# Outer products of the last two pairs of tiles as seven block products, with sums kept in SBUF and three PSUM banks

## The chip, the cores and the metric

The program runs on one core of one Trainium2 chip. The metric is the device time in microseconds (us) of a whole execution. The kernel before took 988.21 us, the median of three runs (985.57 to 989.87).

## The reference

The input is q, k and v of an attention with 8 batches, 8 heads, 576 positions and 64 features per head, and three weight matrices. Keys and values are averaged over groups of 8 positions, so each query sees 72 keys. The attention's output, reshaped to 4608 tokens of 512 features, goes through a gated layer:

```
attn_out = softmax(q @ mean8(k).T / 8) @ mean8(v)      # per head
x = attn_out.transpose(0, 2, 1, 3).reshape(4608, 512)
a = x @ w_a            # 512 -> 1536
b = x @ w_b            # 512 -> 1536
out = (a * b) @ w_out  # 1536 -> 512
```

All is float32. Nearly all of the multiplications lie in the last three lines.

## The kernel before

The 4608 tokens are nine tiles of 512 (`NT`). The 1536 gated features are twelve blocks of 128 (`NF`, index f). Every float32 operand of a matmul is split into a rounded high part and a low part, and a product is three matmuls: high by high, low by high and high by low.

Tiles 0 to 2 are computed one by one. Tiles 3 to 8 form three pairs, (3, 4), (5, 6) and (7, 8), called pairs 0, 1 and 2 here. Within a pair the products x @ w_a and x @ w_b for both tiles are done together by the scheme of Winograd: `both(p, f)` makes seven block products for feature block f (`product`, six matmuls of 512 columns each) in three PSUM banks, and `fold` and `fold_second` combine them. VectorE does five additions and multiplications that read PSUM, ScalarE does two copies out of PSUM, and GpSimd does one addition and one multiplication. The result is a*b for the block f of the first tile (`first`) and of the second (`fifth`).

The outer product (a*b) @ w_out is the plain one in all pairs. For the first tile, `split_gated` parts the gated block into high and low, and `ffn_out` adds four groups of three matmuls into the banks acc0 to acc3; these groups stand between the block products of the next f (`rest`). The gated blocks of the second tile are written to DRAM (`later`). When the pair is through, twelve `ffn_out` of the second tile follow, 144 matmuls, with the blocks fetched back (`fetch_gated`). The sums of x that the next pair needs (`sums_of_x`) are made at that time.

The whole program is put in order at build time. `Schedule` holds chains of operations with estimated durations and ranks. It always starts the operation that can start first, and of those that can start within a small slack the one with the lowest rank. Each engine then runs its queue strictly in that written order, and semaphores hold an instruction back until what it needs is there. DMAs are all issued by SyncE. The lines that issue the work are line 292 (matmuls), 234 (additions and multiplications of VectorE and GpSimd), 256 and 260 (copies of ScalarE) and 271 (DMAs).

Four large SBUF buffers (w0 to w3) hold what is streamed in by `loads`: the block weights of one f (`stream`, tile name j, 1.8 MB in four DMAs), x of the next pair, and w_out for the second tile (tile name wo). A buffer is reused in the order in which it comes free.

Of the kernel before, what the change touches and what calls it, by code (L numbers as in the profile page):

```python
# [19 lines left out]
P = 128  # L20
# [19 lines left out]
BY_HEAD, LESS_MAX, COPIED = range(3)  # L40
EARLY = [BY_HEAD, LESS_MAX, BY_HEAD, LESS_MAX, COPIED, BY_HEAD, BY_HEAD, BY_HEAD]
# [156 lines left out]
def attn_moe_kernel(ctx: ExitStack, tc: tile.TileContext, q, k, kn, v, vn, vr, wa, wb, wo, out):  # L198
# [78 lines left out]

    def pe(calls, rank=None, turn=False):
# [67 lines left out]
    streamed = {("o", t1 * NF + f) for _, t1 in PAIRS for f in range(NF)}  # L346
    stream, combos, temps = {}, {}, []
    jd = [dram.tile([P, 2, NJ + 1, HALF * P], F32, name=f"jd{f}") for f in range(NF)]
    od = [dram.tile([P, 2, DM], F32, name=f"od{f}") for f in range(NF)]
    xd = {t: dram.tile([P, NK, NT], F32, name=f"xd{t}") for t in range(2, NTILE)}  # L350
# [48 lines left out]
    for p, (t0, t1) in enumerate(PAIRS):  # L399
        order += [("both", p, f) for f in range(NF)] + [("rest", p, 0)]  # L400
        order += [("out", t1, f) for f in range(NF)]
    lasting = {"in": 24 * 0.228, "out": 12 * 0.228, "both": 54 * 0.228, "rest": 8 * 0.228}
    due, at = {}, 28.0
    for item in order:
        if item[:2] == ("in", 0):
            at = max(at, 28.0 + 11.5 * item[2])
        due[item] = at
        at += lasting[item[0]]
    ends = {}
# [4 lines left out]
    stored |= {t1 * NF + f for _, t1 in PAIRS for f in range(NF)}  # L414
    uses, upcoming = [], {name: [] for name in ("ab", "o", "h")}
    for kind, t, f in order:
        if kind == "out":
            uses.append(t * NF + f)
        elif kind == "both":
# [218 lines left out]
    def loads():  # L638
        todo = [("x", 0)]
        for p, (t0, t1) in enumerate(PAIRS):  # L640
            todo += [("both", p, f) for f in range(NF)] + [("wo", t1, 0)]
            todo += [("x", p + 1)] if p + 1 < len(PAIRS) else []
            todo += [("wo", t1, c) for c in (1, 2)]
# [4 lines left out]
        for kind, at, *more in todo:  # L648
            tag = yield from take(free_w)
            if kind == "both":  # L650
# [7 lines left out]
                sch.spawn(freed(tag, ("product", at, f, S4)), 0.0)  # L658
            elif kind == "wo":
# [22 lines left out]
    def sums_of_x(p):  # L682
        yield W(("x", p))
        if p:
            yield W(("pair", p - 1))
# [5 lines left out]
        sch.spawn(all_temps(p, two), 0.0)  # L691
        rank = due["both", p, 0] - 12.0
        lead = rank - (SOON if not p else 0.0)
# [28 lines left out]
    def all_temps(p, two):  # L722
        if not temps:
            yield W(("split", "h", STD * NF - 1))
            yield from take(hs)
        temps[:] = [x[:, c * NT:(c + 1) * NT] for x in two for c in range(2)]
        temps.extend(place(sb, [P, NT], F32, tag, f"temp_{tag}_{p}") for tag in ("p2", "h"))
        mark("temps", p)
# [452 lines left out]
    def fold(p, f, u, v, r, first, third, fourth, fifth):  # L1181

        t0 = PAIRS[p][0]
        yield W(("product", p, f, X00))
        if f > 1:
            yield W(("split", "h", t0 * NF + f - 2))
        else:
# [28 lines left out]
        yield from split_gated(t0 * NF + f, first)  # L1216
        mark("folded", p, f)

    def fold_second(p, f, third, fourth, fifth):
# [6 lines left out]
        mark("second", p, f, 1)  # L1226
        later[x] = dram.tile([P, NT], F32, name=f"later_{x}")
        yield dma(later[x], fifth)
        mark("stored", x)

    waiting = []

    def both(p, f):
# [9 lines left out]
        first, third, fourth, fifth = temps[f % 2], temps[2], temps[3], temps[4 + f % 2]  # L1243
# [14 lines left out]
        def rest(n):  # L1258
            if f > 1 or f == 1 and n > 1:
                yield from waiting.pop(0)  # L1260

# [4 lines left out]
        if not f:  # L1266
# [7 lines left out]
        yield from product(u, A1, X01, start=False)  # L1274
        yield before_r
        yield from product(r, T3, S3)
        yield from rest(1)
        yield W(("fold", p, f, 1))
        yield from product(v, T1, S1)
        yield W(("fold", p, f, 2))  # L1280
        yield from product(r, T4, X11)
        yield from rest(2)
        yield W(("fold", p, f, 3))
        yield from product(v, B1, S4, start=False)
        yield from rest(3)
        waiting.extend(ffn_out(t0, f, (c,)) for c in range(NT // P))
# [22 lines left out]
    def main():  # L1309
        yield W(("first_ins",))  # L1310
        for kind, t, f in order:
# [9 lines left out]
            elif kind == "rest":  # L1321
# [3 lines left out]
                mark("pair", t)  # L1325

    with tc.manual_schedule():
# [18 lines left out]
        for kind, t, f in order:  # L1346
# [10 lines left out]
            elif kind == "both":  # L1357
                sch.spawn(load_weight("o", x), due[kind, t, f])
# [6 lines left out]
        sch.spawn(more_tmps(), 0.0)  # L1365
# [55 lines left out]
```

## Time and profile before

| | |
|---|---|
| median of three runs | 988.21 us |
| the profiled execution's own time | 987.53 us |
| its span, first to last instruction | 985.7 us |
| TensorE (PE) busy | 968.0 us, 98% |
| VectorE (DVE) busy | 560.6 us, 57% |
| ScalarE (ACT) busy | 387.9 us, 39% |
| GpSimd (POOL) busy | 126.4 us, 13% |
| mean granted TensorE clock | 0.997 |
| moved by DMA | 255.66 MB, 259 GB/s |

The busy time of an engine is the sum of its instructions, overlaps counted once. The chain that ended last names, step by step, what the work that came last was waiting for. Times in rows are microseconds from the span's start. Pair 0 runs from about 412 to 620 us, pair 1 from 620 to 800 us and pair 2 from 800 to 982 us. In each, the first 144 to 170 us are the block products with the first tile's outer product, and the last 36 us are the second tile's outer product.

### The profile page before, as it was taken

The numbers are of one execution on the slowest core, as the hardware profiler recorded it, in microseconds if no ns is written. First come the engines' busy times: TensorE is split into PE (matmuls) and PEld (weight loads), VectorE is DVE, ScalarE is ACT, GpSimd is POOL, SyncE is SP. The second block draws the span as 40 slices with busy tenths as digits, with TensorE's granted clock in tenths as the row PEclk, the third lists the DMA queues.
The fourth block names the chain that finished last, engine by engine and source line by source line (L and its number), as shares of the span: only waits on it lengthen the run. The fifth ranks groups of instructions, "written<-read, shape, count | busy, mean of one in ns | idle before, by whom it ended". The sixth has DMA issues, their size and how long they took to land.

```text
span 985.7 us, 12862 instructions
## 1 busy us (share of the span) xinstructions
PE 968.0 (98%) x4568; PEld 801.7 (81%) x4568; DVE 560.6 (57%) x928; ACT 387.9 (39%) x796; POOL 126.4 (13%) x109
## 2 busy tenths in 40 slices
PE   6899999999999999999999999999999999999998
PEld 5688888888888888888888878888888878888876
DVE  6898899888587943858433356333333923333331
ACT  5788666454565533644321133211111621111131
POOL 1002000000000000011212223222222212222210
PEclk9899999999999999999999999999999999999999
DMA  7798999999889998587566876766668967666791
GB/s 269 263 313 295 300 329 295 322 321 319 296 296 305 308 311 279 167 283 237 171 197 215 270 261 230 240 214 216 216 214 303 362 216 234 210 225 210 239 349 74
DMA packets 120655, 255.66 MB, mean 259 GB/s; under 512 B 10192, under 2 KB 26576, under 8 KB 120592
## 3 DMA queue, kind: packets, MB, share of 16 engines
q1 hardware_dynamic: 120592, 254.84, 77.3%
q8 instruction: 36, 0.59, 0.2%
q14 instruction: 27, 0.22, 0.1%
HBM read 195.30 MB, written 59.51 MB: 258 GB/s over the span
## 4 chain that ended last, share of the span: by engine, by line
PE 92%; DMA 4%; ACT 2%; DVE 1%; issue 1%; SPq 0%; ACTq 0%
PE acc L292 29%; PE bank_psb L292 15%; PE bank_psa L292 10%; PE bank_att L292 10%; PE psb L292 9%; PE psa L292 9%; PE po L292 4%; PE psc L292 4%; PE ptr L289 1%; PE pvp L292 1%; DMA j<-jd 1%; DMA jd<-sums_high 1%; DMA kraw<-in_kn 1%; DMA q<-in_q 0%; DMA vraw<-in_vn 0%
## 5 line engine op out<-in xcount | busy, mean ns | idle before, releaser
L292 PE MATMUL bank_psb<-x,j 128*128 128x512 f32 x648 | 165.3, 390 | 0.7 <-DMA j<-jd 0.7
L292 PEld LDWEIGHTS bank_psb<-x,j 128*128 128x128 f32 x648 | 121.0, 188 | 26.3 <-DVE temp L234 1.1
L292 PE MATMUL acc<-jo_later,hh 128*128 128x512 f32 x384 | 122.3, 400 | 0.3
L292 PE MATMUL bank_att<-x,j 128*128 128x512 f32 x432 | 110.4, 391 | 0.0
L292 PE MATMUL bank_psa<-x,j 128*128 128x512 f32 x432 | 110.2, 390 | 0.0
L292 PE MATMUL psb<-xh,jab 128*128 128x512 f32 x288 | 100.7, 398 | 0.0
L234 DVE TENSOR_TENSOR temp<-bank_psb,temp 128x512 f32<-128x512 f32 x72 | 49.8, 692 | 89.1 <-PE bank_psb L292 88.8
L292 PE MATMUL psa<-xh,jab 128*128 128x512 f32 x288 | 99.4, 398 | 0.8 <-ACT vdiag L256 0.8
L292 PEld LDWEIGHTS bank_psa<-x,j 128*128 128x128 f32 x432 | 80.8, 188 | 16.8
L292 PEld LDWEIGHTS bank_att<-x,j 128*128 128x128 f32 x432 | 80.6, 188 | 16.7
L234 DVE TENSOR_TENSOR temp<-bank_psa,temp 128x512 f32<-128x512 f32 x54 | 37.3, 691 | 90.2 <-PE bank_psa L292 89.6
L234 DVE TENSOR_TENSOR temp<-bank_att,temp 128x512 f32<-128x512 f32 x54 | 37.3, 692 | 88.8 <-PE bank_att L292 88.2
L292 PEld LDWEIGHTS acc<-jo_later,hh 128*128 128x128 f32 x384 | 69.8, 188 | 13.9 <-ACT hh L256 1.6
L292 PE MATMUL acc<-jo_later,hl 128*128 128x512 f32 x192 | 75.4, 393 | 0.2 <-DVE hl L234 0.2
L234 POOL TENSOR_TENSOR temp_p<-temp_p,temp 128x512 f32<-128x512 f32 x36 | 46.8, 1301 | 217.2 <-ACT temp_p L256 212.4
L256 ACT CAST hh<-temp 128x512 fp32r<-128x512 f32 x36 | 22.4, 623 | 128.9 <-DVE temp L234 128.9
L234 POOL TENSOR_TENSOR temp_h<-temp_h,temp 128x512 f32<-128x512 f32 x36 | 46.9, 1303 | 181.4 <-ACT temp_h L256 175.3
L292 PEld LDWEIGHTS psa<-xh,jab 128*128 128x128 f32 x288 | 54.1, 188 | 12.6 <-ACT vdiag L256 1.7
L292 PEld LDWEIGHTS psb<-xh,jab 128*128 128x128 f32 x288 | 54.1, 188 | 10.7
L292 PE MATMUL acc<-jo_open,hh 128*128 128x512 f32 x192 | 61.6, 402 | 0.4 <-ACT s L264 0.4
L292 PE MATMUL psb<-xl,jab 128*128 128x512 f32 x144 | 56.3, 391 | 0.0
L292 PE MATMUL psa<-xl,jab 128*128 128x512 f32 x144 | 56.2, 390 | 0.0
(144 smaller groups left out, 1608.6 us busy)
## 6 DMA issues: line engine op xcount, KB each, us to landing
j<-jd SPq DMA_DIRECT2D x108, 512.0 KB, 5.5
jo_later<-od SPq DMA_DIRECT2D x48, 512.0 KB, 3.8
wo<-od SPq DMA_DIRECT2D x36, 512.0 KB, 7.0
jab<-jd SPq DMA_DIRECT2D x34, 512.0 KB, 6.2
jd<-jab SPq DMA_DIRECT2D x24, 512.0 KB, 4.9
back<-later SPq DMA_DIRECT2D x43, 256.0 KB, 5.9
out<-y SPq DMA_DIRECT2D x36, 256.0 KB, 6.0
j<-jd SPq DMA_DIRECT2D x36, 256.0 KB, 4.4
```

The source lines that it names most:

```text
L234: run = lambda e: vec[e].tensor_tensor(out=out, in0=in0, in1=in1, op=op)
L256: return act(out, in_, lambda: nc.scalar.copy(out, in_), rank)
L289: nc.tensor.transpose(to, lhs, rhs)
L292: nc.tensor.matmul(to, lhs, rhs, start=start, stop=stop, skip_group_check=bool(skip))
```

## The change

For pairs 1 and 2 (`PAIRED_OUT`) the outer product is also done for both tiles at once by seven block products, over two feature blocks (2j and 2j+1) at a time. Pair 0 stays as it was.

- The weights: in the time of pair 0, `sums_of_pairs` reads w_out back, forms four sums of its blocks for each of the six j, parts them into high and low and stores them in DRAM (`wd`). In pairs 1 and 2 `loads` streams them, seven DMAs for each j (tile name w), through the same four buffers.
- The gated blocks: `sums_of_gated` makes four sums out of the gated blocks of both tiles and two f, and parts seven of them into high and low (tile names combos), by ScalarE and VectorE.
- The matmuls: `out_piece` does one block product for one half (m) of the output features, three matmuls. There are 14 such pieces for each j. Weights are the stationary operand, so the outputs come out transposed, and the host transposes them back. In even f nothing stands between the block products of `both`; in odd f up to two pieces stand behind each.
- The sums over j: three of the 14 pieces are summed in the banks acc0, acc1 and acc2. The other eleven alternate between two banks, and `add_piece` adds each to a sum in SBUF (VectorE; for j = 0 ScalarE copies).
- The end of a pair: `give_pair` forms the outputs with 14 additions and stores them.
- Gone in pairs 1 and 2: `split_gated`, the way of the second tile's gated block through DRAM, the 144 matmuls behind the pair, and the wait of the next pair's `sums_of_x` for the pair before.

In matmuls, each of the two pairs had 288 for the outer product (24 groups of 12) and now has 252 (6 times 14 times 3).

The core of the diff:

```diff
+PAIRED_OUT = 1, 2
+PAIR_MARGIN, GIVE_MARGIN = 0.5, 6.0
...
 def sums_of_x(p):
         yield W(("x", p))
-        if p:
+        if p and p - 1 not in PAIRED_OUT:
             yield W(("pair", p - 1))
...
             if not p:
                 yield W(*free_at.get(home[c], [last_in]))
+            elif p - 1 in PAIRED_OUT:
+                yield W(("product", p - 1, NF - 1, c))
...
+    out_order = [(c, m) for c in (X00, S2, X01, S3, S1, X11, S4) for m in range(2)]
+    kept_banks = {(X01, 0): "acc0", (X01, 1): "acc1", (X11, 0): "acc2"}
...
+    def sums_of_pairs():
...
+            yield tt(w0, w0, other, ALU.add, (SV, SG), rank)
...
+            yield tt(w1, w1, other, ALU.add, (SV, SG), rank)
+            yield tt(other[:, low], w0[:, high], w0[:, low], ALU.subtract, (SV, SG), rank)
+            yield tt(other[:, high], w1[:, high], w0[:, high], ALU.subtract, (SV, SG), rank)
+            yield tt(w0[:, low], w1[:, high], other[:, low], ALU.subtract, (SV, SG), rank)
+            yield tt(w0[:, high], w1[:, low], w0[:, low], ALU.subtract, (SV, SG), rank)
+            for n, x in enumerate((other, w0)):
+                hi, lo = four[:, 2 * n], four[:, 2 * n + 1]
+                yield copy(hi, x, rank)
+                yield low_part(lo, x, hi, (SV, SG), rank)
...
+    def sums_of_gated(p, j):
...
+        yield tt(s1, x10, x11, ALU.add)
+        yield tt(s2, s1, x00, ALU.subtract)
+
+        def parted(c, src):
+            slot = yield from take(combo_slots)
+            yield copy(slot[0], src)
+            yield low_part(slot[1], src, slot[0])
...
+        yield from parted(X00, x00)
+        yield from parted(S2, s2)
+        yield from parted(X01, x01)
+        yield tt(x10, x00, x10, ALU.subtract)
+        yield from parted(S3, x10)
+        yield tt(x01, x01, s2, ALU.subtract)
+        yield from parted(S1, s1)
+        yield from parted(X11, x11)
+        yield from parted(S4, x01)
...
+    def out_piece(p, j, c, m):
+        yield W(("gated", p, j, c))
...
+        if kept:
+            to, start, stop = lasts[c, m], not j, j == NF // 2 - 1
+        else:
+            tag = yield from take(pair_banks)
+            to, start, stop = bank(tag, f"pair_{p}_{j}_{c}_{m}"), True, True
+        yield pe([(to, w[:, 0], hi, start, False), (to, w[:, 0], lo, False, False), (to, w[:, 1], hi, False, stop)])
...
+    def add_piece(p, j, c, m, src, tag):
+        at = sums_at[c, m]
+        if j:
+            yield W(("added", p, j - 1, c, m))
+            yield tt(at, src, at, ALU.add)
+        else:
+            yield copy(at, src)
+        pair_banks.append(tag)
...
+    def give_pair(p, m):
...
+            yield tt(at[to], at[x], at[y], ALU.add, (SV,) if in_psum(at[x]) else (SV, SG))
...
     def both(p, f):
...
+        def piece():
+            for _ in range(1 if (p, f) == (len(PAIRS) - 1, NF - 1) else 2):
+                if p in PAIRED_OUT and pieces and pieces[0][0] <= p * NF + f:
+                    yield from pieces.pop(0)[1]
...
         yield from product(u, A0, X00)
+        yield from piece()
         yield before_v
         yield from product(v, T2, S2)
+        yield from piece()
...
+        if p in PAIRED_OUT:
+            if f % 2:
+                lag = 3 if f == 1 and p - 1 in PAIRED_OUT else 2
+                pieces.extend((p * NF + f + lag, out_piece(p, f // 2, c, m)) for c, m in out_order)
+            return
...
-        sch.spawn(more_tmps(), 0.0)
+        sch.spawn(attention_over(), 0.0)
+        sch.spawn(sums_of_pairs(), 0.0)
+        sch.spawn(late_places(), 0.0)
```

How the written order changes is shown at three places. The first is TensorE's queue in pair 2, from the fourth block product of f = 3 on. Before, a group of the first tile's outer product (acc) stands between the block products (bank):

```order
L292 MATMUL bank_psb<-x_3_5416,j_3_5729 128x512 [waits DVE_49]
L292 MATMUL bank_psb<-x_3_5416,j_3_5729 128x512 x5
L292 MATMUL bank_psa<-x_2_5476,j_3_5729 128x512 [waits DMAHW5_49,DVE_49]
L292 MATMUL bank_psa<-x_2_5476,j_3_5729 128x512 x5
L292 MATMUL acc_0_5737<-jo_later,hh_5842 128x512 [waits DMAHW4_49]
L292 MATMUL acc_0_5737<-jo_later,hh_5842 128x512
L292 MATMUL acc_0_5737<-jo_later,hl_5843 128x512
L292 MATMUL bank_psb<-x_6_5499,j_3_5729 128x512 [waits Activation_49]
L292 MATMUL bank_psb<-x_6_5499,j_3_5729 128x512 x5
```

After, at the turn from f = 8 to f = 9 of the same pair, where pair_3_... are pieces of j = 3:

```order
L300 MATMUL bank_psb<-x_3_6912,j_8_7701 128x512 [waits DVE_49]
L300 MATMUL bank_psb<-x_3_6912,j_8_7701 128x512 x5
L300 MATMUL bank_att_4119<-x_2_6932,j_8_7701 128x512 [waits DMAHW7_49,DVE_49]
L300 MATMUL bank_att_4119<-x_2_6932,j_8_7701 128x512 x5
L300 MATMUL bank_psb<-x_6_6952,j_8_7701 128x512 [waits Activation_49]
L300 MATMUL bank_psb<-x_6_6952,j_8_7701 128x512 x5
L300 MATMUL bank_att_4119<-x_0_6828,j_9_7888 128x512 [waits DMAHW7_49,DVE_49]
L300 MATMUL bank_att_4119<-x_0_6828,j_9_7888 128x512 x5
L300 MATMUL pair_3_0_0_7919<-combos_work,w_3_7765 128x512 [waits DMAHW0_49]
L300 MATMUL pair_3_0_0_7919<-combos_work,w_3_7765 128x512 x2
L300 MATMUL pair_3_0_1_7923<-combos_work,w_3_7765 128x512 x3
```

In an even f the block products now follow each other with nothing between them; in an odd f they have two pieces behind each.

The second place is VectorE's queue at the turn from pair 1 to pair 2 in the new kernel, when TensorE is in block f = 0 of pair 2. Here combos are the parted gated blocks of pair 1, late_p, late_h and s_2_0 are the fold of pair 2, and x_6 is the part of x for the seventh block product. Before, this queue held only the five operations of the fold here:

```order
L234 TENSOR_TENSOR temp_2_6565<-bank_psb,temp_2_6565 128x512 [waits PE_49,Activation_49]
L234 TENSOR_TENSOR temp_2_6566<-bank_att_4112,temp_2_6565 128x512 [waits DVE_49,PE_49]
L234 TENSOR_TENSOR temp_2_6566<-bank_att_4112,temp_2_6566 128x512 [waits DVE_49,PE_49]
L234 TENSOR_TENSOR temp_2_6565<-bank_psb,temp_2_6565 128x512 [waits PE_49]
L234 TENSOR_TENSOR temp_2_6565<-bank_psa,temp_2_6565 128x512 [waits DVE_49]
```

Now it holds:

```order
L237 TENSOR_TENSOR s_2_0_6966<-bank_psb,s_2_0_6966 128x512 [waits PE_49,Activation_49]
L237 TENSOR_TENSOR hl_1_5_6978<-hh_1_5_6977,kv_1_10_6734 128x512 [waits DVE_49]
L237 TENSOR_TENSOR combos_jo<-kv_1_10_6734,combos_jo 128x512 [waits Activation_49]
L237 TENSOR_TENSOR late_p_5502<-bank_att_4119,s_2_0_6966 128x512 [waits DVE_49,PE_49]
L237 TENSOR_TENSOR combos_jo<-hl_1_5_6978,combos_jo 128x512 [waits Activation_49]
L237 TENSOR_TENSOR combos_x_5755<-tmp_1_11_6818,combos_x_5755 128x512 [waits Activation_49]
L237 TENSOR_TENSOR late_h<-bank_att_4119,late_p_5502 128x512 [waits DVE_49,PE_49]
L237 TENSOR_TENSOR tmp_1_10_6735<-kv_1_10_6734,tmp_1_10_6735 128x512
L237 TENSOR_TENSOR x_6_6952<-x_6596,x_6_6952 128x512
L237 TENSOR_TENSOR combos_x_5755<-tmp_1_10_6735,combos_x_5755 128x512 [waits Activation_49]
```

The part x_6, without which the seventh block product can't run through, now stands behind the fold's fourth result and a sum of gated blocks.

The third place is the end of VectorE's queue. Before, its last instructions part the second tile's gated blocks, and the ends of the outputs are copied out by ScalarE:

```order
L234 TENSOR_TENSOR hl_7822<-back_7760,hh_7821 128x512 [waits DMAHW4_49,PE_49,Activation_49]
L234 TENSOR_TENSOR jo_later<-back_7786,jo_later 128x512 [waits DMAHW7_49,PE_49,Activation_49]
L234 TENSOR_TENSOR hl_7860<-back_7804,hh_7859 128x512 [waits DMAHW0_49,PE_49,Activation_49]
L234 TENSOR_TENSOR jo_later<-back_7823,jo_later 128x512 [waits DMAHW3_49,PE_49,Activation_49]
L234 TENSOR_TENSOR hl_7892<-back_7841,hh_7891 128x512 [waits DMAHW5_49,PE_49,Activation_49]
```

After, it ends with the adding of the last pieces (pair_5_...) and the additions of `give_pair`:

```order
L237 TENSOR_TENSOR sums_tmp_5786<-pair_5_2_1_8315,sums_tmp_5786 128x512 [waits PE_49]
L237 TENSOR_TENSOR sums_work<-last_acc_5789,sums_work 128x512
L237 TENSOR_TENSOR sums_tmp_5787<-pair_5_6_0_8321,sums_tmp_5787 128x512 [waits PE_49]
L237 TENSOR_TENSOR sums_tmp_5788<-pair_5_6_1_8326,sums_tmp_5788 128x512 [waits PE_49]
L237 TENSOR_TENSOR sums_tmp_5782<-sums_tmp_5782,sums_work 128x512 [waits DVE_49]
L237 TENSOR_TENSOR sums_work<-sums_work,sums_q_5784 128x512 [waits DVE_49]
L237 TENSOR_TENSOR sums_q_5784<-sums_q_5784,sums_tmp_5782 128x512 [waits DVE_49]
L237 TENSOR_TENSOR sums_tmp_5782<-last_acc_5791,sums_tmp_5782 128x512 [waits DVE_49]
L237 TENSOR_TENSOR sums_tmp_5787<-sums_tmp_5787,sums_work 128x512
L237 TENSOR_TENSOR sums_work<-last_acc_5790,sums_work 128x512 [waits Pool_49]
```

Eleven additions now stand behind the last one that waits for TensorE. From the end of the last block product of pair 2 on, TensorE's new queue holds 22 pieces and VectorE's holds 44 instructions.

## Rows read from the trace of the kernel before

**Rows 1.** The page: busy time of the engines, and the shares of the chain that ended last.

```profile
PE 968.0 (98%) x4568; PEld 801.7 (81%) x4568; DVE 560.6 (57%) x928; ACT 387.9 (39%) x796; POOL 126.4 (13%) x109
...
PE 92%; DMA 4%; ACT 2%; DVE 1%; issue 1%; SPq 0%; ACTq 0%
```

**Rows 2.** Busy time by stretch: us, then PE, PEld, DVE, ACT and POOL busy (instructions), PE's granted clock, DMA share, GB/s. The stretches are pair 0, then the block products and the second tile's outer product of pair 1, the beginning of pair 2, its block products, its outer product, and the end.

```profile
424.00:584.00 160.00, 159.90 (x758) 132.74 (x756) 74.23 (x123) 43.37 (x91) 31.63 (x24) 1.00 0.70 230
...
640.00:764.00 124.00, 124.00 (x547) 102.21 (x545) 42.30 (x62) 18.45 (x31) 25.90 (x20) 1.00 0.71 232
764.00:800.00 36.00, 35.90 (x157) 29.21 (x157) 23.53 (x31) 17.51 (x27) 6.47 (x4) 1.00 0.78 284
800.00:816.00 16.00, 15.26 (x68) 12.37 (x67) 4.84 (x7) 3.12 (x6) 2.57 (x2) 1.00 0.94 315
...
830.00:946.00 116.00, 115.89 (x511) 95.47 (x510) 39.60 (x58) 17.57 (x30) 25.92 (x20) 1.00 0.71 237
946.00:982.00 36.00, 35.98 (x156) 28.99 (x156) 8.56 (x13) 10.97 (x19) 0.00 (x0) 1.00 0.46 167
982.00:985.70 3.70, 0.00 (x0) 0.00 (x0) 0.00 (x0) 0.59 (x1) 0.00 (x0) 1.00 0.60 226
```

**Rows 3.** The chain that ended last, in order of time (start, us, what): the first block product of pair 1, a group of three outer matmuls, the waits at the ends of the pairs, and the last step.

```profile
619.64 1.36 PE bank_psa L292 x6
621.00 1.36 PE bank_psb L292 x6
...
759.98 0.69 PE acc L292 x3
...
764.19 36.12 PE acc L292 x156
...
803.98 7.81 DMA j<-jd
...
945.86 36.13 PE acc L292 x156
981.99 0.02 issue
982.01 0.59 ACT y L260
```

**Rows 4.** VectorE in order of time at the end of pair 1: start, duration, instruction, and in brackets what it waited for. The second row uses the first row's result; the fourth and fifth are independent of what stands before them.

```profile
762.07 0.69 DVE L234 TENSOR_TENSOR temp<-bank_psb,temp 128x512 f32<-128x512 f32 x1 [1.30 <-PE bank_psb L292]
762.79 0.69 DVE L234 TENSOR_TENSOR temp<-bank_att,temp 128x512 f32<-128x512 f32 x1
764.17 0.69 DVE L234 TENSOR_TENSOR hl<-temp,hh 128x512 fp32r<-128x512 f32 x1 [0.69 <-ACT hh L256]
764.78 0.69 DVE L234 TENSOR_TENSOR hl<-back,hh 128x512 fp32r<-128x512 f32 x1
765.38 0.69 DVE L234 TENSOR_TENSOR jo_later<-back,jo_later 128x512 fp32r<-128x512 f32 x1
```

**Rows 5.** Groups of instructions, shapes kept apart: line, engine, operation, out<-in, count, busy us, mean ns of one, idle before.

```profile
L234 POOL TENSOR_TENSOR temp_h<-temp_h,temp 128x512 f32<-128x512 f32 x36 | 46.9, 1303 | 181.4 <-ACT temp_h L256 175.3 <-DVE temp L234 6.1
...
L256 ACT CAST hh<-temp 128x512 fp32r<-128x512 f32 x36 | 22.4, 623 | 128.9 <-DVE temp L234 128.9
...
L234 DVE TENSOR_TENSOR sums_low<-wab,sums_low 128x256 f32<-128x256 f32 x24 | 10.2, 424 | 0.7
...
L256 ACT COPY temp<-bank_att 128x512 f32<-128x512 f32 x18 | 10.6, 588 | 4.6 <-PE bank_att L292 4.3
```

**Rows 6.** VectorE and GpSimd (POOL) at work at the same time on tiles in SBUF, in order of time, while x of pair 2 is parted.

```profile
775.06 5.01 POOL L234 TENSOR_TENSOR x<-x,x 128x512 fp32r<-128x512 f32 x3 [1.91 <-ACT x L256]
775.43 3.48 DVE L234 TENSOR_TENSOR x<-x,x 128x512 fp32r<-128x512 f32 x2
778.84 1.78 DVE L234 TENSOR_TENSOR hl<-back,hh 128x512 fp32r<-128x512 f32 x1
```

**Rows 7.** The waits of VectorE for DMAs over the whole span (us in total, times, longest), and one of them in pair 0, in order of time.

```profile
DVE vp L249 <- DMA vraw<-in_v: 11.9, 8, 4.4
...
441.20 1.33 DVE L249 TENSOR_REDUCE vp<-vraw 128x64 f32<-128x512 f32 x2 [2.48 <-DMA vraw<-in_v]
```

**Rows 8.** DMA issues over the whole span: count, KB each, median us from issue to landing.

```profile
j<-jd SPq DMA_DIRECT2D x108, 512.0 KB, 5.5
...
j<-jd SPq DMA_DIRECT2D x36, 256.0 KB, 4.4
```

**Rows 9.** TensorE's granted clock in three early stretches (columns as in rows 2).

```profile
30.00:35.00 5.00, 4.54 (x16) 3.77 (x17) 3.75 (x6) 3.24 (x7) 0.00 (x0) 0.50 0.92 314
...
40.00:45.00 5.00, 4.16 (x22) 2.77 (x21) 4.78 (x8) 3.32 (x7) 0.00 (x0) 1.00 0.95 292
45.00:50.00 5.00, 3.51 (x20) 2.60 (x19) 4.10 (x9) 2.22 (x4) 0.00 (x0) 1.00 0.90 311
```

**Rows 10.** TensorE in order of time: the same kind of group, two vdiag matmuls and one vrem, before that fall of the clock and in it.

```profile
23.80 0.59 PE L292 MATMUL po<-early_p,vdiag 128*128 128x256 f32 x2
24.04 0.47 PE L292 MATMUL po<-early_p,vrem 96*128 96x256 f32 x1
24.35 0.60 PE L292 MATMUL po<-early_p,vdiag 128*128 128x256 f32 x2
...
32.83 1.06 PE L292 MATMUL po<-p,vdiag 128*128 128x256 f32 x2
33.32 0.78 PE L292 MATMUL po<-p,vrem 96*128 96x256 f32 x1
33.89 1.05 PE L292 MATMUL po<-p,vdiag 128*128 128x256 f32 x2
```

More of the change, by code (lines that the diff above doesn't have):

```diff
@@ L349, in attn_moe_kernel @@
     od = [dram.tile([P, 2, DM], F32, name=f"od{f}") for f in range(NF)]
+    wd = [dram.tile([P, 2, NJ - T1, BLOCK], F32, name=f"wd{j}") for j in range(NF // 2)]
     xd = {t: dram.tile([P, NK, NT], F32, name=f"xd{t}") for t in range(2, NTILE)}
@@ L400, in attn_moe_kernel @@
         order += [("both", p, f) for f in range(NF)] + [("rest", p, 0)]
-        order += [("out", t1, f) for f in range(NF)]
+        if p not in PAIRED_OUT:
+            order += [("out", t1, f) for f in range(NF)]
     lasting = {"in": 24 * 0.228, "out": 12 * 0.228, "both": 54 * 0.228, "rest": 8 * 0.228}
@@ L408, in attn_moe_kernel @@
         at += lasting[item[0]]
+        if item[0] == "both" and item[1] in PAIRED_OUT:
+            at += 9 * 0.228
     ends = {}
@@ L418, in attn_moe_kernel @@
             uses.append(t * NF + f)
-        elif kind == "both":
+        elif kind == "both" and t not in PAIRED_OUT:
             uses.append(PAIRS[t][0] * NF + f)
@@ L1229, in fold_second @@
         mark("stored", x)
+    late, gated, pair_w, pieces = [], {}, {}, []
+    raw_h, pair_banks, sums_at, lasts = [], [], {}, {}
+    combo_slots, sum_temps = [], []
+    out_order = [(c, m) for c in (X00, S2, X01, S3, S1, X11, S4) for m in range(2)]
+    part_of = {X00: A0, S2: T2, X01: A1, S3: T3, S1: T1, X11: T4, S4: B1}
+    kept_banks = {(X01, 0): "acc0", (X01, 1): "acc1", (X11, 0): "acc2"}
+    def sums_of_pairs():
+        yield W(last_in)
+        four = place(sb, [P, 4, NT], F32R, "x7", "pair_sums")
+        tags = []
+        for _ in range(3):
+            tag = yield from take(tmps, 2)
+            tags.append(tag)
+        low, high = slice(BLOCK), slice(BLOCK, DM)
+        for j in range(NF // 2):
+            yield W(("kept", "o", 2 * j), ("kept", "o", 2 * j + 1), ("product", 0, j + j // 2, X00))
+            rank = due["both", 0, j + j // 2] + 5.0
+            w0, w1, other = [tmp(tag, f"pair{j}_{tag}") for tag in tags]
+            yield clear(PAIR_MARGIN, w0, w1, other)
+            yield dma(w0, od[2 * j][:, 0], rank)
+            yield dma(other, od[2 * j][:, 1], rank)
+            yield dma(w1, od[2 * j + 1][:, 0], rank)
+            yield until_ready(PAIR_MARGIN, w0, other)
+            yield tt(w0, w0, other, ALU.add, (SV, SG), rank)
+            yield clear(0.7, other)
+            yield dma(other, od[2 * j + 1][:, 1], rank)
+            yield until_ready(PAIR_MARGIN, w1, other)
+            yield tt(w1, w1, other, ALU.add, (SV, SG), rank)
[7 more added lines that the diff above has]
+                yield low_part(lo, x, hi, (SV, SG), rank)
+            yield until_ready(PAIR_MARGIN, four)
+            for n in range(2):
+                hi, lo = four[:, 2 * n], four[:, 2 * n + 1]
+                for h, part in enumerate((hi, lo)):
+                    yield dma(wd[j][:, h, 2 * n:2 * n + 2].rearrange("p c s -> p (c s)"), part.bitcast(F32), rank)
+            mark("paired", j)
+        tmps.extend(tags)
@@ new lines, in out_piece @@
+    def out_piece(p, j, c, m):
+        yield W(("gated", p, j, c))
+        yield lambda: (p, j) in pair_w
+        if not j and p - 1 in PAIRED_OUT:
+            yield W(*(("given", p - 1, n, t, half) for n in range(2) for t in PAIRS[p - 1] for half in range(2)))
+        hi, lo = parts["pair", p, j, c]
+        w = pair_w[p, j][:, :, part_of[c], m * P:(m + 1) * P]
+        kept = (c, m) in kept_banks
+        if kept:
[4 more added lines that the diff above has]
+        yield pe([(to, w[:, 0], hi, start, False), (to, w[:, 0], lo, False, False), (to, w[:, 1], hi, False, stop)])
+        mark("piece", p, j, c, m)
+        if j == NF // 2 - 1 and c == X00:
+            sch.spawn(give_pair(p, m), -0.6)
+        if not kept:
+            sch.spawn(add_piece(p, j, c, m, to, tag), -0.8)
+        if m:
+            combo_slots.append(parts.pop(("pair", p, j, c)))
+        if (c, m) == out_order[-1]:
+            mark("pair_out", p, j)
@@ L1242, in both @@
         u, v, r = three_banks if f % 2 == 0 else three_banks[::-1]
-        first, third, fourth, fifth = temps[f % 2], temps[2], temps[3], temps[4 + f % 2]
+        if p in PAIRED_OUT:
+            gated[p, f] = []
+            for _ in range(2):
+                tag = yield from take(raw_h)
+                gated[p, f].append((tag, place(sb, [P, NT], F32, tag, f"{tag}_{p}_{f}")))
+            (_, first), (_, fifth) = gated[p, f]
+            third, fourth = late
+            if f % 2:
+                sch.spawn(sums_of_gated(p, f // 2), -0.7)
+        else:
+            first, third, fourth, fifth = temps[f % 2], temps[2], temps[3], temps[4 + f % 2]
         sch.spawn(fold(p, f, u, v, r, first, third, fourth, fifth), -1.0)
@@ L1320, in main @@
                 yield from both(t, f)
-            elif kind == "rest":
+            elif kind == "rest" and t not in PAIRED_OUT:
                 while waiting:
@@ L1325, in main @@
                 mark("pair", t)
+        while pieces:
+            yield from pieces.pop(0)[1]
     with tc.manual_schedule():
```

144 lines of the change are left out of this document (130 added, 14 removed).

## The prediction

> **What bounds the kernel now.** I read the page's busy times and chain first, then the busy time by stretch, then the chain and VectorE's rows around the ends of the pairs. TensorE is busy 98% of the span and has 92% of the chain [rows 1]. In the stretches of pairs 1 and 2 it is never without work to speak of: 124.00 of 124.00 us, 115.89 of 116.00, 35.90 of 36.00, always at clock 1.00 [rows 2]. So a matmul that goes gives its whole time back, as long as TensorE stays the bound. VectorE has room on the average (42.30 of 124 us while the block products run [rows 2]), and little follows TensorE's last matmul: one copy of 0.59 us at 982.01, and the stores until 985.70 [rows 2, 3]. That last point decides here.
>
> What a matmul costs: a block product of six takes 1.36 us, an outer group of three 0.69 [rows 3]. As a check, pairs 1 and 2 hold 168 block products and 192 groups: 168 x 1.36 + 192 x 0.69 = 361.0 us. From 619.64 that ends at 980.6; the trace has 981.99 [rows 3], so some 1.4 us were waits, 0.7 of them in the stretch with the wait for weights [rows 2, 3].
>
> **The change part by part.** *Matmuls.* 84 pieces for a pair instead of 96 groups; 24 groups of three fewer, 24 x 0.69 = 16.6 us off TensorE. Nothing else on TensorE changes: a piece has the shape of a group.
>
> *The end of pair 2.* Before, 144 matmuls of the second tile (most of 36 us [rows 3]) stood behind the last fold and hid it, and VectorE was nearly idle (8.56 of 36 us [rows 2]). Now, when the last block product ends, TensorE has 22 pieces left (22 x 0.69 = 15.2 us), and VectorE has 44 instructions, each 128x512 and float32, that nothing else can take, one after another in a written order: two of the fold, 18 additions of pieces, 4 sums of gated blocks, 7 low parts, 13 of the outputs. All take 0.69, but they overlap: an independent one starts 0.61 us after the one ahead (764.17, 764.78, 765.38), one that needs the result ahead 0.72 (762.07, 762.79) [rows 4]. Ten of the 44 wait for VectorE itself: 34 x 0.61 + 10 x 0.72 = 27.9 us. Going through the two queues by hand (a piece's bank comes free only when the addition two pieces before is through) VectorE stands still for about 1.2 us more, twice behind a piece, once behind a ScalarE cast (0.62 [rows 5]) and once behind the one addition that GpSimd has (1.30 [rows 5]). So VectorE needs 29 us where TensorE needs 15.2: 14 us of the 16.6 go back here. Bounds: 44 x 0.61 = 26.8 if nothing ever waits, 44 x 0.72 = 31.7 if all depend.
>
> The last block product of pair 2 ends at 619.64 + 168 x 1.36 + (168 - 22) x 0.69 = 948.9 if TensorE never waits. VectorE ends at 978.0. The last store takes what it took before from its copy's end on, 985.70 - 982.60 = 3.1 us [rows 2, 3]: 981.1.
>
> *The regular blocks.* In an even f TensorE has 7 x 1.36 = 9.5 us and no group between the products. VectorE's order puts up to six operations on gated blocks between the folds. I went through f = 8 of pair 2: the fold's second result is there 0.4 us before the product that waits for it, the fourth 0.45. For two blocks VectorE has 10 of the fold, 11 of the pieces and 11 of the gated blocks, 32 x 0.61 to 0.72 = 19.5 to 23.0 us, GpSimd four of 1.30, TensorE 7 x 2 x 1.36 + 14 x 0.69 = 28.7. I take no loss; the other end is the third rival. ScalarE (11 casts and copies of 0.6 us) is far from full.
>
> *From pair 1 to pair 2.* The second tile's 36 us, in which x of the next pair was summed and parted (VectorE 23.53 us [rows 2]), are gone, so this work lies beside f = 11 of pair 1 and f = 0 of pair 2. By hand f = 11 just holds it (26 VectorE instructions, 16 to 19 us, in 19.2). In f = 0 there are 15 in 9.5 us, and GpSimd parts three more pieces of x and does the fold's two, 5 x 1.3 to 1.7 [rows 5, 6]. The part x_6 comes 1.4 us too late for the seventh product, more if GpSimd is in between: I take 1.5, from 0 to 5. Queued behind it is the pair's first fold, and TensorE is what waits.
>
> *Pair 0.* 48 more operations in SBUF (24 of 0.69, 24 of 0.42 [rows 5]) are some 27 us for VectorE, which had 74.23 of 160 busy [rows 2]. Twelve of them wait for DMAs, in order, with folds queued behind. The nearest rows are the waits of the averages: 8 waits, 11.9 us, one of 2.48 in this very stretch, and TensorE was busy all the same (159.90 of 160.00) [rows 2, 7]. I take 0.5, from 0 to 5.
>
> *Streams.* For two blocks 3 x 1.8 MB in 28.7 us are 192 GB/s, under the 237 of before [rows 2]. But a buffer for w leaves fewer ahead: at f = 10 of pair 1 (x of pair 2 holds one more) w and j have to come within some 11 us, and 3.7 MB at the 315 GB/s of the busiest stretch here [rows 2] take 11.7. w moves in parts of 256 KB, median 4.4 us against 5.5 for 512 [rows 8]. TensorE waited 0.74 us behind such a load before [rows 2, 3]; I take 0.5 for two such places together, from 0 to 4.
>
> *Sum.* 981.1 + 1.5 + 0.5 + 0.5 = 983.6 us of span against 985.7. The profiled execution's own time is 1.8 above its span, and the median 0.7 above that: 986.1, I say 986. All lower ends: 981.1 - 2.3 = 978.8, in the median 981.3. All upper ends: 981.1 + 2.6 + 14 = 997.7, in the median 1000.2.
>
> **The rivals.** A difference under 0.5%, 4.9 us, is about what a measurement of this kernel can't tell from none, so faster means below 983.3 and slower above 993.2.
>
> *The end is shorter and nothing waits (faster).* For it: VectorE's independent instructions do start every 0.61 us [rows 4], and the average load leaves room. Against it: 44 instructions in a row have no cover, whatever the rest does. Without waits 981.1 of span, 983.6 in the median; with the end's lower bound 981.3. I put it at 981.5.
>
> *VectorE and GpSimd shut each other out (slower).* When both work in SBUF they don't run side by side: three GpSimd additions took 5.01 us instead of 3 x 1.30, two of VectorE 3.48 and one 1.78 instead of 0.69 [rows 5, 6]. The Trainium skill has this as a rule, in "SBUF — State Buffer" on the shared port pair: it is an exclusive lock, whoever starts first keeps it for the whole instruction, and a VectorE instruction counts if it has two SBUF inputs. The rows agree with it. In an even f VectorE now has six or seven such operations between its folds and GpSimd two; before there was one. If one GpSimd addition (1.30) gets in front of such an operation ahead of a fold, the margin of 0.4 us is short by 0.9. That decides from where it happens in most of the twelve even blocks: 12 x 0.9 = 11 us, 986.1 + 11 = 997. Against it: folds read PSUM, and those next to GpSimd's work kept 0.69 in the rows.
>
> *TensorE's clock falls at the end (slower).* There TensorE works only half of the time, in bits. In the start of the program the granted clock was 0.50, the 1.2 GHz level, from 30 to 35 us, behind a stretch of small matmuls with gaps, and the same kind of group took 1.06 us from start to start instead of 0.55 [rows 9, 10]. At that rate 22 pieces take 30 us, and the last additions follow: about 39 instead of 29 us, 996. Against it: at 40 to 50 us TensorE was busy 70 to 83% with gaps and kept 1.00 [rows 9].
>
> "TensorE: Matmul & The Clock Gate" of the Trainium skill (the clock gate) says that the lower level is the default and activity lifts it; this rival is what that rule would do here.
>
> **How the numbers follow.** The sum as worked out: 0.46, with a range of its own of 982.5 to 990. Nothing waits: 0.37. Lock: 0.12. Clock: 0.05. Of the first, 0.03 lie below 983.3. Faster 0.40, same 0.43, slower 0.17. The range leaves out about 0.1 at each end: 979.5, a little under all lower ends, to 995.
>
> **What would show it.** Right, if TensorE holds 4,496 matmuls; if from the last block product (six matmuls into bank_psb) to VectorE's last instruction there are 28 to 30 us with VectorE without pause, and TensorE with gaps; if TensorE's even blocks in pairs 1 and 2 come every 28.7 us in twos; and if f = 0 of pair 2 has a wait of 1 to 3 us behind VectorE. If TensorE is done within 1 or 2 us of VectorE having its last outer sum, my end is wrong. If waits behind VectorE stand in every even f, with GpSimd's additions over 1.5 us, the lock decides. A clock of 0.5 in the last 30 us shows the third. A wait of several us for w or j behind a DMA would show that I was wrong on the streams.

## The result and the profile after

The changed kernel takes 993.73 us, the median of ten runs (990.88 to 995.79); the kernel before took 988.18 in ten runs beside them. The ratio is 1.0061, with a 95% interval of 1.0046 to 1.0076: slower by 0.6%, where 986.0 was predicted, faster by 0.2%. The time lies inside the stated range of 979.5 to 995.0, but on the other side of no change; the prediction had given 0.17 to more than 993.2. The profiled execution took 995.79 us, with a span of 994.0. It is the slowest of the ten, 2.1 us above the median, so what its trace shows is somewhat more than the median lost.

The page of the changed kernel, busy times and shares of the chain; its rows answer to [rows 1]:

```profile
PE 958.4 (96%) x4496; PEld 790.4 (80%) x4496; DVE 719.2 (72%) x1188; ACT 414.4 (42%) x849; POOL 145.8 (15%) x120
...
PE 89%; DVE 4%; DMA 4%; ACT 2%; SPq 1%; issue 1%; DVEq 0%; ACTq 0%
```

The 4,496 matmuls are there, 72 fewer than before, and TensorE works 9.6 us less. But the chain, which was 92% TensorE, now holds DMA, VectorE and SyncE's queue. TensorE's waits in pairs 1 and 2 and at the end, of the changed kernel (us in total, times, longest):

```profile
PE bank_psb L300 <- DMA j<-jd: 2.6, 1, 2.6
PE bank_psb L300 <- DVE x L237: 2.2, 1, 2.2
PE bank_att L300 <- DMA j<-jd: 1.3, 1, 1.3
PE bank_psa L300 <- ACT pr L259: 1.3, 1, 1.3
...
PE bank_att L300 <- DVE late_h L237: 0.5, 1, 0.5
```

The same view of the kernel before has one row, 0.7 us for j. Five waits stand here, all before the end of the last block product. The same in stretches, in the columns of [rows 2]:

```profile
619.00:628.00 9.00, 6.40 (x23) 4.89 (x22) 0.32 (x1) 2.61 (x5) 0.00 (x0) 0.81 0.85 270
797.00:807.00 10.00, 7.85 (x28) 5.96 (x27) 7.97 (x11) 2.72 (x5) 2.87 (x2) 0.83 0.93 300
812.00:940.00 128.00, 127.53 (x563) 105.28 (x562) 91.18 (x138) 32.90 (x58) 30.48 (x22) 1.00 0.62 200
961.00:994.00 33.00, 18.66 (x66) 12.14 (x64) 28.66 (x44) 3.42 (x6) 1.65 (x1) 0.83 0.17 64
```

In the long middle of pair 2 TensorE is never without work to speak of. The largest losses lie at the starts of the pairs, where the clock is low as well, and at the end, where VectorE (28.66 us, 44 instructions) is the busy one.

The start of pair 1, TensorE and then SyncE's queue (start, duration, idle time before and what ended it):

```profile
620.53 1.52 PE L300 MATMUL bank_psa<-x,j 128*128 128x512 f32 x6
624.64 2.93 PE L300 MATMUL bank_psb<-x,j 128*128 128x512 f32 x6 [2.60 <-DMA j<-jd]
627.37 1.66 PE L300 MATMUL bank_psa<-x,j 128*128 128x512 f32 x6
```

```profile
603.00 1.19 SPq L274 DMA_DIRECT2D j<-jd  x2
619.30 0.34 SPq L274 DMA_DIRECT2D out<-y  x1
619.69 0.52 SPq L274 DMA_DIRECT2D j<-jd  x1
620.31 0.57 SPq L274 DMA_DIRECT2D out<-y  x1
```

The weights j of f = 0 are four DMAs. Two go out at 603.00. The third, which the second block product needs, stands behind the store of an output y of pair 0, and that store waits until 619.30 for y, which ScalarE copies out of a bank. SyncE's waits from 585 to 640 us have it as the longest, 15.0 us:

```profile
SPq L274 <- ACT y L263: 16.8, 3, 15.0
```

The second product begins 2.75 us late (624.64 instead of 620.53 + 1.36) and then takes 2.73 instead of 1.36 us.

The turn from pair 1 to pair 2, TensorE, VectorE and GpSimd:

```profile
798.04 1.07 PE L300 MATMUL bank_psb<-x,j 128*128 128x512 f32 x4
801.26 0.86 PE L300 MATMUL bank_psb<-x,j 128*128 128x512 f32 x2 [2.15 <-DVE x L237]
801.92 2.76 PE L300 MATMUL bank_att<-x,j 128*128 128x512 f32 x6
804.48 1.86 PE L300 MATMUL pair<-combos_jo,w 128*128 128x512 f32 x6
```

```profile
798.24 0.69 DVE L237 TENSOR_TENSOR late_h<-bank_att,late_p 128x512 f32<-128x512 f32 x1 [0.65 <-PE bank_att L300]
798.85 0.68 DVE L237 TENSOR_TENSOR tmp<-kv,tmp 128x512 f32<-128x512 f32 x1
799.45 1.76 DVE L237 TENSOR_TENSOR x<-x,x 128x512 fp32r<-128x512 f32 x1
```

```profile
799.07 1.58 POOL L237 TENSOR_TENSOR s<-s,late_h 128x512 f32<-128x512 f32 x1 [0.26 <-DVE late_h L237]
```

This is the wait that was forecast: the low part of x_6, behind the fold and a sum of gated blocks. It takes 1.76 us, not 0.69, since GpSimd works from 799.07 to 800.65. Again the next product is slow (2.56 us to the one behind it).

The end, VectorE's first two and last two instructions and TensorE's last block product:

```profile
960.85 0.69 DVE L237 TENSOR_TENSOR tmp<-bank_psb,tmp 128x512 f32<-128x512 f32 x1 [1.29 <-PE bank_psb L300]
961.58 0.69 DVE L237 TENSOR_TENSOR tmp<-bank_att,tmp 128x512 f32<-128x512 f32 x1
...
989.56 0.69 DVE L237 TENSOR_TENSOR sums_tmp<-sums_tmp,sums_tmp 128x512 f32<-128x512 f32 x1
990.17 0.68 DVE L237 TENSOR_TENSOR sums_tmp<-sums_tmp,sums_work 128x512 f32<-128x512 f32 x1
```

```profile
959.29 1.52 PE L300 MATMUL bank_psb<-x,j 128*128 128x512 f32 x6
960.65 1.52 PE L300 MATMUL pair<-combos_work,w 128*128 128x512 f32 x6
```

The last block product ends at 960.65, VectorE at 990.85: 30.2 us, where 29 were predicted. The start of it is further off: 948.9 was predicted.

### The profile page after: what moved, and what is told of

Same layout as the page of the kernel before. It is cut to its first block, busy times and chain, and to the rows that moved or that the text cites. A ratio compares the mean times of both kernels' runs of the same rounds, so it can differ in the third digit from the quotient of the medians.

```text
span 994.0 us, 13099 instructions
## 1 busy us (share of the span) xinstructions
PE 958.4 (96%) x4496; PEld 790.4 (80%) x4496; DVE 719.2 (72%) x1188; ACT 414.4 (42%) x849; POOL 145.8 (15%) x120
## 4 chain that ended last, share of the span: by engine, by line
PE 89%; DVE 4%; DMA 4%; ACT 2%; SPq 1%; issue 1%; DVEq 0%; ACTq 0%
PE acc L300 15%; PE bank_psb L300 14%; PE bank_att L300 10%; PE psb L300 9%; PE psa L300 9%; PE bank_psa L300 9%; PE pair L300 8%; PE po L300 4%; PE psc L300 4%; PE last_acc L300 2%; PE ptr L297 1%; DMA j<-jd 1%; PE pvp L300 1%; DVE sums_tmp L237 1%; SPq L274 1%
## 5 line engine op out<-in xcount | busy, mean ns | idle before, releaser
L300 PE MATMUL bank_psb<-x,j 128*128 128x512 f32 x648 | 167.5, 394 | 4.7 <-DMA j<-jd 2.6
L300 PE MATMUL acc<-jo_later,hh 128*128 128x512 f32 x192 | 62.0, 404 | 0.1
L300 PE MATMUL pair<-combos_jo,w 128*128 128x512 f32 x165 | 45.0, 405 | 1.9 <-DVE combos_jo L237 1.1
L300 PE MATMUL po<-p,vdiag 128*128 128x256 f32 (+3 forms) x184 | 45.6, 351 | 0.5 <-ACT p L259 0.5
L300 PE MATMUL psc<-kdiag,q 128*128 128x144 f32 x288 | 45.6, 288 | 0.2
L300 PEld LDWEIGHTS psc<-kdiag,q 128*128 128x128 f32 x288 | 41.4, 190 | 5.1 <-issue 0.7
L300 PE MATMUL pair<-combos_x,w 128*128 128x512 f32 x153 | 39.8, 391 | 0.8 <-DVE sums_tmp L237 0.8
L300 PEld LDWEIGHTS pair<-combos_jo,w 128*128 128x128 f32 x165 | 32.1, 196 | 10.3 <-DVE combos_jo L237 1.4
L300 PEld LDWEIGHTS acc<-jo_open,hh 128*128 128x128 f32 x192 | 34.5, 188 | 6.9 <-ACT s L267 0.8
L300 PEld LDWEIGHTS acc<-jo_later,hh 128*128 128x128 f32 x192 | 34.1, 188 | 6.0 <-ACT hh L259 0.5
```

## The experiments

All ratios are to the kernel before, run on the same chip. Its median was 987.3 to 987.4 us there, against 988.18 beside the changed kernel, so a difference to the changed kernel in microseconds can be off by about 0.9.

**The stores later.** Two lines put the stores of pair 0's last tile later in SyncE's queue:

```diff
         mark("y", t, c)
+        if t == PAIRS[0][1]:
+            yield until_ready(12.0, y)
         yield dma(out[t * NT + c * P:t * NT + (c + 1) * P, :], y)
```

> The four stores of pair 0's last tile (y) are put later in SyncE's written order, so that the weights j of the first two feature blocks of pair 1 no longer stand behind them; nothing else moves on any engine. Theory 1 (the order of SyncE's queue made j late): the wait of 2.6 us before the second block product of pair 1 goes, and with it the 1.37 us that this product took longer behind the wait: 4 us less than the changed kernel, 989.7 us (988.5 to 991). Rival (the streams are too full since the sums of w_out were added, and j would land late however early it is issued): a wait of 1.5 us or more stays at that place, and the time is within 1 us of 993.7.

Measured: 989.96 us, ratio 1.0019 (1.0006 to 1.0031), 3.8 us under the changed kernel. SyncE issues the four j parts of f = 0 one behind the other, all by 606.2 us, and three of f = 1 from 610.7 on, in one row here; TensorE runs through:

```profile
603.09 9.48 SPq L274 DMA_DIRECT2D j<-jd  x7
620.25 0.34 SPq L274 DMA_DIRECT2D out<-y  x1
```

```profile
621.48 1.52 PE L300 MATMUL bank_psa<-x,j 128*128 128x512 f32 x6
622.84 1.52 PE L300 MATMUL bank_psb<-x,j 128*128 128x512 f32 x6
```

So it was the order of the queue, not the bytes. In this execution the wait for j at f = 11 was 0.5 us and not 1.3, so some of the 3.8 us may be from there.

**x first.** The rank of x's parts at the turn to pair 2, -0.65, becomes -0.75, better than the -0.7 of the gated sums.

> In the turn from pair 1 to pair 2 the low parts of x get a better rank than the sums of the gated blocks, on VectorE and GpSimd; nothing moves on TensorE. Theory 1 (x_6 is late because it stands behind gated sums and a fold in VectorE's queue): the wait of 2.15 us before the last two matmuls of the seventh block product goes, with the 1.2 us that the next product and the 0.3 us that the pieces behind it took longer: 3.5 to 4 us less, 990 us (988.5 to 991.5). Rival (VectorE and GpSimd together have too much in this stretch, whatever stands first): waits of 2 us or more appear at other products between 785 and 815 us, for late_h, combos or a bank, and the time is 992.5 to 996.

Measured: 991.66 us, ratio 1.0040 (1.0024 to 1.0056), 2.1 us less, just outside what was expected. The planner now gave both halves of x_6's low part to GpSimd. TensorE at the turn:

```profile
800.50 1.52 PE L300 MATMUL bank_psb<-x,j 128*128 128x512 f32 x6
802.32 1.65 PE L300 MATMUL bank_att<-x,j 128*128 128x512 f32 x6 [0.29 <-DVE late_p L237]
```

The wait of 2.15 us and the low clock are gone, 0.3 us is left. The other 1.5 us that were expected were for the clock behind the wait, and it does not fall in every execution (last section).

**Only the last pair.** `PAIRED_OUT = 2,` instead of `1, 2`.

> Only pair 2 gets the outer product in seven block products; pair 1 is the plain one of before. Theory 1 (the end of the program costs 14.4 us once, each pair gives 8.3 us back, and the waits for j and x in pairs 1 and 2 cost the rest): 988.2 - 8.3 + 14.4 + 0.9 for the sums of w_out in pair 0 = 995.2, up to 999 where j or w come late at the start of pair 2; slower than the changed kernel. From the last block product to VectorE's last instruction 29 to 31 us as before. Rival (the end is not what costs, but the waits and the crowded VectorE in the middle, most of it in pair 1 and at its turn): 981 to 987.

Measured: 999.15 us, ratio 1.0113 (1.0092 to 1.0134), just above the 995.2 to 999 that were expected. With half of the change the kernel is slower than with all of it. From the last block product (end 964.55) to VectorE's last instruction there are 29.2 us:

```profile
963.19 1.52 PE L300 MATMUL bank_psb<-x,j 128*128 128x512 f32 x6
...
993.06 0.68 DVE L237 TENSOR_TENSOR sums_tmp<-sums_tmp,sums_work 128x512 f32<-128x512 f32 x1
```

The rival's 981 to 987 falls, and the end is paid once, as theory 1 has it. What pair 1 gives back after its own waits is 999.15 - 993.73 = 5.4 us; that it is 8.3 without them was not shown. And the theory had the late load at another place: j came late at the start of pair 1, by 3.1 us, though pair 1 is plain there, and not at that of pair 2. Two products behind it ran at the lower clock:

```profile
624.17 2.93 PE L300 MATMUL bank_psb<-x,j 128*128 128x512 f32 x6 [3.07 <-DMA j<-jd]
```

So that wait comes with what is new in pair 0, the sums of w_out, which this kernel keeps, and not with pair 1's new work.

**j before w.** In `loads`, j of f = 11 of pair 1 goes ahead of the seven parts of w for j = 4.

> In pair 1 SyncE issues the weights j of f = 11 ahead of the seven parts of w for j = 4, which are needed one block product later. Theory 1 (at f = 11 j is late because w stands ahead of it in the queue when a buffer comes free): the wait for j there, 1.3 to 2.5 us in the executions so far, falls below 0.3, and no wait for w of more than 0.3 takes its place: 1.5 us less, 992.2 us (990.5 to 993.5), which the trace tells better than the time. Rival (the bytes of j and w together come too late whatever stands first): a wait of 1 us or more for w before the first piece of f = 11, and no gain.

Measured: 994.43 us, ratio 1.0067 (1.0046 to 1.0089), above the 990.5 to 993.5 that were expected. In the trace the wait at f = 11 is gone and none for w stands there, but the time shows no gain. In this execution the wait at the start of pair 1 was 4.0 us; an interval of 0.4% can't tell 1.5 us. What this wait costs in the median stays open.

**The end, plain.** The last two feature blocks of pair 2 get the plain outer product: for each of eight outputs two groups of three matmuls in one bank, then one addition to the sums, which are complete by then.

```diff
+    def out_last(p, n, t, half, m):
...
+        yield pe([(to, w[:, 0], hi, not n, False), (to, w[:, 0], lo, False, False), (to, w[:, 1], hi, False, bool(n))])
...
+    def add_last(p, t, half, m, src, tag):
...
+        yield tt(y, src, y, ALU.add)
```

> The last two feature blocks of pair 2 get the plain outer product, with outputs transposed as well: 16 groups of three in place of 14 pieces, eight additions in place of eleven and of seven low parts four, so that the 14 additions of the outputs can begin in f = 11; two pieces instead of one stand behind each product of f = 11. Nothing ahead of f = 8 of pair 2 moves. Theory 1 (VectorE's 44 instructions behind the last block product are the end's cost): that product ends 7 x 0.69 = 4.8 us later, near 965.5, behind it VectorE has about 20 instructions, 12 to 14 us, and TensorE 16 groups, 11 us; with the store of 3.1 the span is 981 to 983, 12 us less, 982 us in the median (979.5 to 985). Rival (the end is bound by something else, TensorE's clock or GpSimd's additions and the lock with VectorE): less than 6 us are saved, 988 or more, with GpSimd's additions of 1.3 us or more or a clock of 0.5 in the last 20 us.

Measured: 981.71 us, ratio 0.9927 (0.9911 to 0.9942), 12 us less, as expected. The last block product, TensorE's last matmuls and VectorE's last instructions:

```profile
964.42 1.52 PE L300 MATMUL bank_psb<-x,j 128*128 128x512 f32 x6
...
976.02 2.88 PE L300 MATMUL plain<-combos_jo,w_last 128*128 128x512 f32 x12
```

```profile
978.26 1.44 DVE L237 TENSOR_TENSOR sums_tmp<-plain,sums_tmp 128x512 f32<-128x512 f32 x2
```

From 965.78 on VectorE has 17 instructions instead of 44, since some are gone and others run before, and is done at 979.70, 0.8 us after TensorE. The three waits are still in this kernel.

**The three waits together**, with the end of the changed kernel.

> The later stores, the better rank of x and j ahead of w together; the end of pair 2 as in the changed kernel. Theory 1 (three waits with what follows them cost what the prediction lacked): 3.8 + 2.1 us as measured alone and 1.5 for the third, 986.3 us (984.5 to 988), which is the predicted 986.0 within 0.2%, and the last block product ends near 951. Rival (a wait that goes comes back further on, since the buffers and VectorE are full): 989 or more, with a new wait of 2 us or more between 640 and 950 us.

Measured: 988.16 us, ratio 1.0016 (1.0000 to 1.0032), 1.9 us more than the 986.3 expected, between theory 1 (up to 988) and the rival (from 989). The last block product ends at 952.4, where 951 was expected. The waits for j are gone; the one for x_6 is back:

```profile
PE bank_psb L300 <- DVE x L237: 2.2, 1, 2.2
PE bank_psa L300 <- ACT pr L259: 1.3, 1, 1.3
```

It is the old wait at the old place, not a new one as the rival had it: in the written order with j earlier, both halves of x_0's low part are VectorE's, and one half of x_6's is as well, behind late_h again.

**The three waits and the end.**

> The later stores, the better rank of x, j ahead of w, and the plain outer product for the last two feature blocks of pair 2. Theory 1 (waits and end are independent costs): 981.7 as measured with the new end, less the 7.4 us of the three waits: 974.3 us (972 to 977), faster than the kernel before by 1.3%; VectorE's last instruction within 1.5 us of TensorE's last. Rival (with TensorE earlier the weights of pair 2 or x come late in turn): 978 or more.

Measured: 977.51 us, ratio 0.9904 (0.9888 to 0.9919), 3.2 us more than expected and just above the 977 that theory 1 allowed, under the rival's 978. The same wait for x_6, 2.2 us, is there; the other 1.0 us is not accounted for.

**x_6 by GpSimd alone.**

```diff
-                yield low_part(lo[:, n], src[:, n], hi[:, n], (SV, SG))
+                yield low_part(lo[:, n], src[:, n], hi[:, n], (SG,) if c == S4 and p - 1 in PAIRED_OUT else (SV, SG))
```

> As the kernel with three waits and the end, where the wait for x_6 was still there since VectorE had the second half of x_6's low part again; here both halves are written for GpSimd, which had nothing to do before it. Theory 1 (one low part of 0.69 us that VectorE starts late, and that took 1.76 beside GpSimd, is what the seventh product waits for): the wait of 2.15 us goes, none over 0.7 takes its place between 780 and 815 us, and the time is 975.4 us (974 to 976.5) against 977.5. Rival (GpSimd's two parts of 1.3 to 1.75 us push the fold's second result back by as much): a wait of 1 us or more for late_p or late_h, and 976.5 to 979.

Measured: 975.85 us, ratio 0.9888 (0.9872 to 0.9905). All that TensorE waits for from 585 us on:

```profile
PE bank_psa L300 <- ACT pr L259: 1.3, 1, 1.3
PE bank_att L300 <- DVE late_h L237: 1.0, 2, 0.5
PE pair L300 <- DVE sums_work L237: 0.9, 2, 0.5
```

Theory 1 holds by the trace: the wait for x_6 is gone, and the longest wait in that stretch is 0.5 us. The time is 1.7 us less, but the intervals of the two ratios overlap. This version is 1.1% faster than the kernel before.

## Why the prediction was wrong

- **Matmuls.** Right: 24 groups fewer for each pair.
- **The end of pair 2.** Right: 44 instructions, 30.2 us against 29, and 3.1 us for the store. By the prediction's own reckoning (30.2 - 15.2) it gave back 15 of the 16.6 us, not 14; the difference is TensorE's clock (rivals, below). The plain end, which leaves 17 of the 44 instructions behind the last block product, got 12 back.
- **Streams: the step that failed.** The text weighed bytes (3.7 MB in 11 us) and took 0.5 us, from 0 to 4, for two places, of which it named f = 10 of pair 1. What came were 2.75 us at f = 0 of pair 1, with a slow product of 1.37 more behind it, and 1.5 at f = 11 (770.64 instead of 767.78 + 1.36 = 769.14): 5.6 us. This is the sign that the prediction itself had named for being wrong on the streams.

```profile
767.78 1.52 PE L300 MATMUL bank_psb<-x,j 128*128 128x512 f32 x6
770.64 1.62 PE L300 MATMUL bank_att<-x,j 128*128 128x512 f32 x6 [1.34 <-DMA j<-jd]
```

With the stores later the wait at f = 0 goes, and 3.8 us in the median; with 3.8 in place of 0.5 the sum is 989.3 and no longer faster. The late load was readable from the written order of SyncE's queue. Before, j_0 stands whole ahead of the second tile's first store, out<-y_0; now half of it stands behind:

```
before: j_0<-jd, back<-later, out<-y_3, j_0<-jd, j_0<-jd, j_0<-jd, j_1<-jd, jo_later<-od, j_1<-jd, out<-y_0
after:  j_0<-jd, j_0<-jd, out<-y_0, j_0<-jd, out<-y_1, j_0<-jd, j_1<-jd, out<-y_2, j_1<-jd, out<-y_3
```

The prediction shows TensorE's and VectorE's queues gone through by hand, and not SyncE's.
- **From pair 1 to pair 2.** The place and the cause were right, the size was not: 1.5 us taken, 0 to 5 as bounds, 4.05 measured. That is 2.5 us of wait (801.92 instead of 798.04 + 1.36), where GpSimd made the low part 1.07 us longer, and 1.5 us of slow matmuls behind it. With x first the median fell by 2.1 us, which fits that those slow matmuls do not come every time.
- **The regular blocks.** Taken as nothing, 2 us measured. At f = 2 of pair 1 ScalarE's copy out of a bank stood behind a cast that waited for VectorE, and the third product came 1.4 us late; late_h of f = 2 of pair 2 came 0.6 us late for the first product of f = 3 (832.66 instead of 832.03). Both waits stand in all traces with both pairs changed, 1.2 to 1.3 and 0.5 us. The margins of 0.4 us that were worked out for f = 8 were not there in every block.
- **Pair 0.** 0.5 taken; pair 1 began at 620.53 instead of 619.64. In the eight experiments it began between 618.91 and 622.47, so this is not told apart from chance.

Together: 5.6 + 4.05 + 2.05 + 0.9 = 12.6 us against 2.5 taken. The groups of three took 0.68 and not 0.69, 146 x 0.01 = 1.5 less. That leaves 11.1; the last block product came 960.65 - 948.9 = 11.75 late. This is the account of one execution, the slowest.

- **The rivals.** "Nothing waits" fell. The lock of VectorE and GpSimd was real in single instructions (1.76 us at 799.45 and 972.69), but from 812 to 940 us TensorE was busy for 127.53 of 128.00, so it does not decide the even blocks. "SBUF — State Buffer" of the Trainium skill (the shared port pair) has it as an exclusive lock for the whole instruction, and the rows agree: 799.07 + 1.58 = 800.65, then 0.6 us for the addition. The clock fell at the end too, and not without cost. Two stretches of the changed kernel, and the same work in the kernel with only the last pair changed (columns as in [rows 2]):

```profile
973.00:977.00 4.00, 2.39 (x7) 1.28 (x7) 3.86 (x5) 2.16 (x4) 0.90 (x1) 0.85 0.00 0
977.00:981.00 4.00, 4.00 (x14) 3.08 (x13) 3.27 (x5) 0.00 (x0) 0.00 (x0) 0.72 0.00 0
```

```profile
973.00:981.00 8.00, 5.50 (x21) 3.39 (x20) 8.00 (x13) 2.28 (x4) 1.65 (x1) 1.00 0.01 2
981.00:986.00 5.00, 4.59 (x18) 2.98 (x18) 4.91 (x9) 0.00 (x0) 0.00 (x0) 1.00 0.00 0
```

VectorE waits for the slow pieces (3.27 us busy of 4.00). Of the six traces with this end the clock fell in three (the changed kernel, the stores later, the three waits), and VectorE was done 30.2 to 30.3 us behind the last block product; in the other three it was 29.2 to 29.3, at a clock of 1.00. So this rival's mechanism came in half of them, at 1.0 us and not at 10.

The measured time is 993.73 - 986.0 = 7.7 us above the prediction. That j behind the stores, x_6 and the end cost what was read for them is shown by removing them: alone 3.8, 2.1 and 12.0 us, 17.9 together, and the last version, without all three and the wait at f = 11, is 17.9 us under the changed kernel (by the ratios 2.0% and 1.7%). The two waits are 5.9 us, where the sum had 2.0 for them: 3.9 of the 7.7. The rest is read from the traces, as the wait at f = 11, the regular blocks and the clock at the end; what each of these cost in the median was not shown.

## What to carry to other kernels

Where a change moves work between stages, read the queue that issues the transfers as you read the engines: a load that is early enough by its bytes is late when a store that waits for the stage's end stands in front of it. Work at the end of a program has no cover, so count the instructions behind the last large matmul; a plain form with fewer additions can win there, even with more matmuls. And a wait of TensorE costs more than its length, if the clock falls behind it.

## What was not expected of the hardware

Behind a wait of 2 to 4 us TensorE's clock often fell for one or two block products. Stretches of the changed kernel, columns as above (the granted clock is the third number from the end):

```profile
620.00:624.00 4.00, 2.05 (x10) 1.35 (x8) 0.00 (x0) 1.75 (x3) 0.00 (x0) 1.00 0.86 226
624.00:628.00 4.00, 3.35 (x9) 2.69 (x10) 0.32 (x1) 0.00 (x0) 0.00 (x0) 0.57 1.05 381
628.00:632.00 4.00, 4.00 (x19) 3.34 (x18) 1.06 (x2) 0.21 (x1) 0.00 (x0) 1.00 1.06 395
```

From 624 to 628 us it is 0.57 on the average, near 0.50, the 1.2 GHz level, and at 1.00 again, 2.4 GHz, behind it. In all five executions with the wait of 2.6 to 4.0 us at the start of pair 1 it fell (0.72 to 0.86 from 620 to 632 us). Behind the wait of 2.15 us for x_6 it fell in two of six (0.91 from 792 to 812 us in the changed kernel and with j before w; 1.00 in the other four). "TensorE: Matmul & The Clock Gate" of the Trainium skill (the clock gate) says that the lower level is that of an idle engine, and the rows agree, since it fell behind waits; why it fell only in some executions behind the same wait no row shows. The prediction had used it for the end of the program alone, and not behind the waits it forecast.
